# A new table for the order of work in a clustered-attention and feed-forward kernel on one core

## The chip, the cores and the metric

One Trainium2 chip (trn2), one core. The metric is the device time of one execution in microseconds (us). The inputs have fixed shapes and the program runs one launch.

## What is computed

The reference, cut to what matters:

```python
q_n, k_n, c_n = q/|q|, k/|k|, centroids/|centroids|            # q, k, v: [4, 8, 768, 64]
q_assign = argmax(q_n @ c_n.T); k_assign = argmax(k_n @ c_n.T)  # 16 clusters per head
scores = where(q_assign == k_assign, q @ k.T / 8, -1e9)
x = softmax(scores) @ v                                         # tokens x (heads * 64) = 3072 x 512
h = x @ w_in                                                    # 3072 x 2048
g = (a0 + a1*h + a2*h*h + a3*h*h*h) / (1 + |b0|*|h| + |b1|*h*h + 1e-6)
out = g @ w_out                                                 # 3072 x 512
```

## The kernel before

Work is tiled by batch b (0 to 3), head pair (0 to 3, two heads of 64 fill 128 partitions) and token block tb (0 to 2, 256 tokens each). Values that must keep more than 16 bits are split into a high and a low fp16 part, and TensorE (PE) adds the cross products.

- `load` steps: the weights come once, in 32 loads `rwi`, `rwo` through a ring of two buffers, and VectorE (DVE), ScalarE (ACT) and GpSimd (POOL) turn them into the resident fp16 pairs `win` and `wout`. This lies beside the attention of batch 0.
- `v_scale` loads the values of a batch once more (`rvm`, through the same two buffers) and squares them on ACT for a scale that only the batch's own feed-forward needs.
- `prep` loads a head pair's queries and keys (`rq`, `rk`), splits them (`tq`, `tk`), turns them by DMA into `sq` and `sk` (L1018), multiplies with the centroids into `ptl` (L1050), and builds the cluster marks on DVE: `mx`, `df`, `mxi`, `oh` (L1064 to L1074).
- `attend`, once per 128 tokens and head: scores `s` on PE (L1154), their scaling and row maximum on DVE (L1183), the exponential on ACT, the reciprocal of the sum on DVE (L1202), the split into `ah` on ACT (high) and DVE (low, L1214), the turn by DMA (L1221), and the product with the values, `px` (L1234), from which `x` comes. Batch 0 has a variant of its own, `attend_keys` (scores L1278 and L1322, product L1341).
- `moe`, once per batch and token block: for four chunks ci and two halves h, PE forms `ph` (two steps of 12 matmuls, L1441) in one of two PSUM buffers, ACT writes `u` = |h| scaled and `t`, DVE makes the polynomial in `t` (L1458, L1459) and so frees `ph`; POOL squares (`s`, L1505 and L1506), ACT takes Ln and Exp of it (L390, the helper of all its activations), the quotient is put together (L1517 or L1528, L1541, L1546), ACT casts the high part (L1550), the low part follows (L1554), and PE adds `po` (L1565). After four chunks ACT scales `po` into `ob`, and a DMA stores it. In batch 3 the low part and one more product run on DVE (`ed.3`, `gld.3` in the table K), and the second half's `u`, `t`, `s` tiles lie in space that attention lent: they are called `sq1`, `sk1`, `sq2` there and print as `sq`, `sk`, `sq`.

Every step is recorded with `plan.op` (L43); its engine name, its nanoseconds and its due time are dropped, and only the function that issues its instructions is kept. `emit` then runs the 4,184 functions in the order of the table `ORDER` (L61 to L244):

```python
    def emit(self):
        assert sorted(ORDER) == list(range(len(self.ops)))
        for i in ORDER:
            self.ops[i]()
```

Each engine, and SyncE (SP), which issues all loads, stores and turns, works off its own instructions in the order in which they were issued. So the table sets five queues at once, and with them the order in which the buffers of each ring change hands. A step at the head of a queue that must wait holds up all behind it on that engine.

Of the kernel before, what the change touches and what calls it, by code (L numbers as in the profile page):

```python
# [246 lines left out]
def clustered_attention_moe_kernel(  # L247
# [97 lines left out]

    def ring(dt, name):
        return buf([P, FW], dt, "ring", name, NR)

# [1306 lines left out]
```

## Time and profile before

| What | Value |
|---|---|
| median of 3 runs | 938.6 us (938.35 to 940.33) |
| the profiled execution | 938.91 us |
| its span, first to last instruction | 937.1 us |
| mean granted TensorE clock | 0.988 of full |
| busy: PE, DVE, ACT, POOL | 865.3, 840.7, 813.4, 729.5 us |
| DMA queue with the kernel's own transfers | 72.3% of 16 engines' span, 136.39 MB |

The profiled execution lies 0.31 us above the median, and 1.81 us of it lie outside the span. A page gives the busy time of each engine; matmuls overlap, so busy time of PE is a union of overlapping spans. The views used below are: stretches of time with the busy time of each engine in each, the instructions of one engine in order of time with the idle time before each in brackets and what ended it, the chain of work that ended last, and the waits by who waited for whom. "L390" is the line of the helper that issues every activation.

### The profile page before, as it was taken

The numbers are of one execution on the slowest core, as the hardware profiler recorded it, in microseconds if no ns is written. First come the engines' busy times: TensorE is split into PE (matmuls) and PEld (weight loads), VectorE is DVE, ScalarE is ACT, GpSimd is POOL, SyncE is SP. The second block draws the span as 40 slices with busy tenths as digits, with TensorE's granted clock in tenths as the row PEclk, the third lists the DMA queues.
The fourth block names the chain that finished last, engine by engine and source line by source line (L and its number), as shares of the span: only waits on it lengthen the run. The fifth ranks groups of instructions, "written<-read, shape, count | busy, mean of one in ns | idle before, by whom it ended". The sixth has DMA issues, their size and how long they took to land.

```text
span 937.1 us, 20745 instructions
## 1 busy us (share of the span) xinstructions
PE 865.3 (92%) x7705; PEld 583.9 (62%) x7705; DVE 840.7 (90%) x1503; ACT 813.4 (87%) x1558; POOL 729.5 (78%) x771
## 2 busy tenths in 40 slices
PE   2679998888999998999999999999999999998997
PEld 1357665665666666666666666666576765776663
DVE  6888989758989899999999999999999998998886
ACT  5577786999999999999999999999899998985764
POOL 3556788988999999989989898988878985454431
PEclk9989999999999999999999999999999999999999
DMA  7997755799867799988889888899787585610000
GB/s 224 240 205 149 213 138 162 190 206 205 163 121 153 151 155 199 189 145 165 156 153 175 155 158 168 158 176 192 141 154 145 103 154 113 106 29 12 12 24 22
DMA packets 360852, 137.70 MB, mean 147 GB/s; under 512 B 335664, under 2 KB 352048, under 8 KB 360752
## 3 DMA queue, kind: packets, MB, share of 16 engines
q1 hardware_dynamic: 360752, 136.39, 72.3%
q8 instruction: 60, 0.98, 0.4%
q14 instruction: 40, 0.33, 0.1%
HBM read 41.98 MB, written 6.29 MB: 52 GB/s over the span
## 4 chain that ended last, share of the span: by engine, by line
PE 51%; DVE 20%; ACT 11%; DMA 8%; issue 5%; POOL 4%; SPq 1%; ACTq 0%; DVEq 0%; POOLq 0%
PE ph L1441 17%; PE po L1565 16%; PE s L1154 6%; PE px L1234 6%; DVE ah L1214 3%; DVE s L1183 3%; DMA rwi<-in_moe_w_in_dram 2%; DVE t L1546 2%; ACT s L390 2%; DVE t L1458 2%; ACT u L390 1%; DVE t L1459 1%; DMA rvm<-in_v_dram 1%; DVE top L1287 1%; ACT ah L390 1%
## 5 line engine op out<-in xcount | busy, mean ns | idle before, releaser
L1441 PE MATMUL ph<-x,win 128*128 128x256 f16 x2304 | 274.0, 274 | 7.7 <-DVE t L1459 5.8
L1441 PEld LDWEIGHTS <-win 128*128 128x128 f16 x2304 | 225.2, 98 | 56.7 <-DVE t L1459 7.5
L1565 PE MATMUL po<-wout,s 128*128 128x512 f16 x1008 | 240.2, 380 | 0.1
L1565 PEld LDWEIGHTS <-s 128*128 128x128 f16 x1008 | 96.9, 98 | 102.4 <-issue 4.5
L1183 DVE TENSOR_SCALAR_CACHE_REDUCE s<-s,cc 128x768 f32<-128x768 f32 x144 | 146.3, 1019 | 15.9 <-PE s L1154 14.7
L1214 DVE SCALAR_TENSOR_TENSOR ah<-s,su,ah 128x768 f16<-128x768 f32 x144 | 144.4, 1010 | 2.8 <-ACT ah L390 2.3
L390 ACT ACTIVATE ah<-s,su 128x768 f16<-128x768 f32 x144 | 128.6, 901 | 8.9 <-DVE su L1202 8.3
L390 ACT ACTIVATE s<-s,nm 128x768 f32<-128x768 f32 x144 | 126.1, 876 | 8.1 <-DVE s L1183 6.2
L1154 PE MATMUL s<-sk,sq 128*128 128x384 f16 x576 | 117.4, 328 | 9.8 <-DVE ah L1214 8.1
L1506 POOL TENSOR_TENSOR s<-s,u 128x512 f32<-128x512 f32 x84 | 113.4, 1350 | 7.0
L1505 POOL TENSOR_SCALAR s<-u,g 128x512 f32<-128x512 f32 x84 | 71.9, 856 | 47.0 <-ACT u L390 32.8
L1528 POOL TENSOR_TENSOR s<-s,u 128x512 f32<-128x512 f32 x72 | 96.7, 1344 | 7.5 <-ACT u L390 7.1
L1554 POOL TENSOR_TENSOR s<-t,s 128x512 f16<-128x512 f32 x72 | 88.2, 1227 | 10.8 <-ACT s L1550 10.7
L1546 DVE SCALAR_TENSOR_TENSOR t<-s,t 128x512 f32<-128x512 f32 x84 | 85.1, 1014 | 0.5 <-POOL s L1528 0.4
L1154 PEld LDWEIGHTS <-sq 128*128 128x128 f16 x576 | 51.9, 98 | 54.0 <-DVE ah L1214 18.4
L1234 PE MATMUL px<-at,vhi 128*64 128x256 f16 x864 | 75.0, 275 | 1.5 <-DVE t L1459 1.0
L1459 DVE SCALAR_TENSOR_TENSOR t<-t,gk,ph 128x512 f32<-128x512 f32 x84 | 62.8, 748 | 3.0
L390 ACT ACTIVATE t<-ph,gk 128x512 f32<-128x512 f32 x84 | 65.4, 780 | 0.0
L390 ACT ACTIVATE u<-ph,gk 128x512 f32<-128x512 f32 x84 | 57.6, 686 | 7.1 <-PE ph L1441 6.5
L1458 DVE SCALAR_TENSOR_TENSOR t<-ph,gk,t 128x512 f32<-128x512 f32 x84 | 62.2, 741 | 1.0 <-ACT t L390 0.7
L1234 PE MATMUL px<-at,vlo 128*64 128x256 f16 x432 | 60.0, 273 | 0.0
L1535 POOL TENSOR_TENSOR t<-t,u 128x512 f32<-128x512 f32 x43 | 56.8, 1321 | 4.0 <-ACT u L390 0.6
(232 smaller groups left out, 1754.4 us busy)
## 6 DMA issues: line engine op xcount, KB each, us to landing
rwi<-in_moe_w_in_dram SPq DMA_DIRECT2D x16, 512.0 KB, 3.8
rwo<-in_moe_w_out_dram SPq DMA_DIRECT2D x16, 512.0 KB, 4.3
rk<-in_k_dram SPq DMA_DIRECT2D x32, 192.0 KB, 3.2
rq<-in_q_dram SPq DMA_DIRECT2D x32, 192.0 KB, 3.7
rvm<-in_v_dram SPq DMA_DIRECT2D x16, 384.0 KB, 4.1
rv<-in_v_dram SPq DMA_DIRECT2D x16, 384.0 KB, 4.3
...
```

The costliest lines, as they stand in the source:

```text
L390: lambda: nc.scalar.activation(out=out(), in_=in_(), func=func, **{a: (x() if callable(x) else x) for a, x in kw.items()}),
L1154: nc.tensor.matmul(sc.ap[:, i, :SH], lhsT=st["q" + x].ap[:, j, t, :], rhs=st["k" + x].ap[:, j, ks, :].rearrange("p t c -> p (t c)"), start ...
L1183: lambda nm=nm, view=view: ts(out=view(), in0=view(), scalar1=cc.ap[:, 0:1], scalar2=None, op0=ALU.mult, op1=ALU.min, accum_out=nm.ap),
L1214: lambda part=part, view=view, su=su: stt(out=part(1), in0=view(), scalar=su.ap, in1=part(0), op0=ALU.mult, op1=ALU.subtract),
L1234: nc.tensor.matmul(px.ap[j * D : (j + 1) * D, :], lhsT=vv.ap[:, j, kt, :], rhs=at[j].ap[:, p_, kt].rearrange("p t c -> p (t c)"), start=(i ...
L1441: nc.tensor.matmul(ph.ap[:, fi * TW : (fi + 1) * TW], lhsT=win[:, wpart, c, f * P : (f + 1) * P], rhs=xs[c].ap[:, xpart], start=(i == 0), ...
L1458: stt(out=t[h].ap, in0=ph.ap, scalar=col("rho")(), in1=t[h].ap, op0=ALU.mult, op1=ALU.mult)
L1506: nc.gpsimd.tensor_tensor(out=sv(), in0=sv(), in1=uv(), op=ALU.mult)
L1528: lambda uv=uv, sv=sv: nc.gpsimd.tensor_tensor(out=sv(), in0=sv(), in1=uv(), op=ALU.mult),
L1546: lambda tv=tv, sv=sv: stt(out=tv(), in0=sv(), scalar=2.0, in1=tv(), op0=ALU.subtract, op1=ALU.mult),
L1554: lambda tv=tv, g16=g16, e=(nc.vector if kshare("gld", b, i_) else nc.gpsimd): e.tensor_tensor(out=g16(1), in0=tv(), in1=g16(0), op=ALU.su ...
L1565: nc.tensor.matmul(po[ti].ap, lhsT=g16(gg)[:, c0 : c0 + P], rhs=wout[:, wpart, f, :], start=(i == 0 and f == 0), stop=(i == 2 and f == NF ...
```

## The change

The table `ORDER` is replaced by another permutation of the same 4,184 steps. Its first line, old and new:

```diff
-3 377 376 28 375 4 5 374 6 7 40 8 9 1 379 381 382 29 383 32 30 10 388 31 391 380 34 33 392 41 384 44 42 489
...
+3 376 377 28 375 374 4 5 6 40 7 8 0 9 379 381 382 10 29 383 32 30 388 31 391 380 33 34 392 44 384 41 490 42
```

Besides, the nanoseconds that each step is recorded with are others (a weight load 2000 in place of 1460, a load of values 1500 for 1100, of queries or keys 800 for 1100, and some compute steps by a few per cent). `Plan.op` drops them, so the program does not hold them. Code behind four new switches (`mw`, `swing`, `atc`, `fine`) is added; none of them is in the table K, whose line is unchanged, so it takes the path of before:

```diff
-    def dma(ns, out, in_, r, w, vt, chain=None):
-        op("SP", ns, lambda: nc.sync.dma_start(out=out(), in_=in_()), r, w, vt, co=w, chain=chain)
+    def dma(ns, out, in_, r, w, vt, chain=None, claim=()):
+        op("SP", ns, lambda: nc.sync.dma_start(out=out(), in_=in_()), r, w, vt, claim=claim, co=w, chain=chain)
...
-            raw = buf([P, 2 * FW], I32, "wraw", "r" + n, 2)
-            dma(1460, lambda raw=raw: raw.ap, lambda src=src: src.bitcast(I32), [], [raw], vt - kn("wd", 3))
+            raw = load([P, 2 * FW], I32, "r" + n)
+            dma(2000, lambda raw=raw: raw.ap, lambda src=src: src.bitcast(I32), [], [raw], vt - kn("wd", 3))
...
-                        (750, 1280)[k] if last else (900, 1600)[k],
+                        (750, 1280)[k] if last else (930, 1780)[k],
```

Each engine has the same compute and DMA instructions in both programs; the waits between engines follow from the order. 227 of the 4,184 steps keep their place in the table; a step is moved by 12 places on average. Lines below L345 of the changed file stand 5 to 11 further down than before.

Three places, as the queues stand before and now. The first is SP, from the second value load of batch 1's scale to the loads of its third head pair: `sk11_1` and `sq11_1` are the turned keys and queries of head pair 1 of batch 1, `rvm2_0` and `rvm2_1` values of batch 2 for its scale, `rk1_2` keys of the next pair. Before:

```order
L404 DMA rvm2_0_2645<-in_v_dram 128x2x384
L1026 DMA sk21_0_2537<-sk11_0_2181 64x1536
L404 DMA rv1_0_2657<-in_v_dram 128x2x384
L1018 DMA_TRANSPOSE sk11_1_2692<-tk11_1_2300 128x12x128
L404 DMA rvm2_1_2702<-in_v_dram 128x2x384
L1018 DMA_TRANSPOSE sq11_1_2709<-tq11_1_2454 128x12x128
```

Now:

```order
L409 DMA rk1_2_2679<-in_k_dram 128x384
L409 DMA rvm2_0_2690<-in_v_dram 128x2x384
L1026 DMA_TRANSPOSE sq11_1_2696<-tq11_1_2466 128x12x128
L1026 DMA_TRANSPOSE sk11_1_2703<-tk11_1_2324 128x12x128
L409 DMA rvm2_1_2709<-in_v_dram 128x2x384
```

The two turns now follow each other, and the value load that stood between them stands behind both.

The second is DVE where the first feed-forward steps begin: `t0_0_0_0` and `t0_0_0_1` are the polynomials of the first two `ph`, `mxi1_1` and `oh1_1` the cluster marks of head pair 1 of batch 1, `ah` and `s` its attention. Before:

```order
L1073 TENSOR_REDUCE mxi1_1_2956<-df1_1_2890 128x24
L1183 TENSOR_SCALAR s1_0_1_1_2940,nm1_0_1_1_2976<-s1_0_1_1_2940,cc1_0_1787 128x2x384
L1202 RECIPROCAL su1_0_1_0_2915<-su1_0_1_0_2915 128x1
L1074 TENSOR_TENSOR oh1_1_2988<-df1_1_2890,mxi1_1_2956 128x384
L1458 SCALAR_TENSOR_TENSOR t0_0_0_0_2985<-ph0_0_0_0_2896,gk0_2308,t0_0_0_0_2985 128x512
L1459 SCALAR_TENSOR_TENSOR t0_0_0_0_2985<-t0_0_0_0_2985,gk0_2308,ph0_0_0_0_2896 128x512
L1002 SCALAR_TENSOR_TENSOR tk11_2_2883<-rk1_2_2728,ksc1_2_2948,tk11_2_2883 128x12x64
L1202 RECIPROCAL su1_0_1_1_3002<-su1_0_1_1_3002 128x1
L1214 SCALAR_TENSOR_TENSOR ah1_0_1_0_3041<-s1_0_1_0_2872,su1_0_1_0_2915,ah1_0_1_0_3041 128x768
L1214 SCALAR_TENSOR_TENSOR ah1_0_1_1_3047<-s1_0_1_1_2940,su1_0_1_1_3002,ah1_0_1_1_3047 128x768
L953 TENSOR_SCALAR qsc1_2_3067<-sumq1_2_2974 128x1
L1183 TENSOR_SCALAR s1_0_2_1_3057,nm1_0_2_1_3069<-s1_0_2_1_3057,cc1_0_1787 128x2x384
```

Now:

```order
L1191 TENSOR_SCALAR s1_0_1_1_2947,nm1_0_1_1_2962<-s1_0_1_1_2947,cc1_0_1777 128x2x384
L1222 SCALAR_TENSOR_TENSOR ah1_0_1_0_2958<-s1_0_1_0_2877,su1_0_1_0_2917,ah1_0_1_0_2958 128x768
L961 TENSOR_SCALAR qsc1_2_2997<-sumq1_2_2937 128x1
L1467 SCALAR_TENSOR_TENSOR t0_0_0_0_2980<-ph0_0_0_0_2897,gk0_2307,t0_0_0_0_2980 128x512
L1468 SCALAR_TENSOR_TENSOR t0_0_0_0_2980<-t0_0_0_0_2980,gk0_2307,ph0_0_0_0_2897 128x512
L1010 SCALAR_TENSOR_TENSOR tk11_2_2912<-rk1_2_2679,ksc1_2_2953,tk11_2_2912 128x12x64
L1210 RECIPROCAL su1_0_1_1_2983<-su1_0_1_1_2983 128x1
L1191 TENSOR_SCALAR s1_0_2_0_3003,nm1_0_2_0_3035<-s1_0_2_0_3003,cc1_0_1777 128x2x384
L1467 SCALAR_TENSOR_TENSOR t0_0_0_1_3029<-ph0_0_0_1_2964,gk0_2307,t0_0_0_1_3029 128x512
L1468 SCALAR_TENSOR_TENSOR t0_0_0_1_3029<-t0_0_0_1_3029,gk0_2307,ph0_0_0_1_2964 128x512
L1222 SCALAR_TENSOR_TENSOR ah1_0_1_1_3051<-s1_0_1_1_2947,su1_0_1_1_2983,ah1_0_1_1_3051 128x768
```

The marks (`mxi1_1`, `oh1_1`) have left this place; they stand 14 and 15 steps further down. Between the two polynomials stood two `ah` and one `s` step of the attention; now one `ah` stands ahead of the first polynomial, the other behind the second, and one `s` step, of another row of tokens, is left between them. On PE the score step of `s1_0_2_0` has come ahead of the third `ph` (`ph0_0_1_0`), that of `s1_0_2_1` has gone behind the first half of the fourth (`ph0_0_1_1`), and the first product `px1_0_0` stands 6 steps further down. On ACT the squares of two `rvm` loads of batch 2 (steps 2217 and 2219 of the table) stand 27 and 30 steps further down.

The third is ACT in batch 3, where the last chunk of token block 0 ends: `sq13_0_3`, `sk13_0_3`, `sq23_0_3` are its `u`, `t`, `s`, and the cast into `sq23_0_3` is what the last `po` of the block waits for; `sq23_1_0` belongs to the next block. Before:

```order
L390 ACTIVATE sq13_1_0_12350<-ph3_1_0_1_12296,gk3_8970 128x512
L390 ACTIVATE sk13_1_0_12353<-ph3_1_0_1_12296,gk3_8970 128x512
L390 ACTIVATE sq23_1_0_12355<-sq23_1_0_12355,cq_76 128x512
L390 ACTIVATE u3_2_0_0_12393<-ph3_2_0_0_12336,gk3_8970 128x512
L390 ACTIVATE t3_2_0_0_12399<-ph3_2_0_0_12336,gk3_8970 128x512
L1550 CAST sq23_0_3_12260<-sk13_0_3_12263 128x512
```

Now:

```order
L395 ACTIVATE sq13_1_0_12296<-ph3_1_0_1_12236,gk3_9080 128x512
L395 ACTIVATE u3_1_0_0_12249<-s3_1_0_0_12251,cq_76 128x512
L1560 CAST sq23_0_3_12207<-sk13_0_3_12194 128x512
L395 ACTIVATE u3_1_3_0_12332<-ph3_1_3_0_12281,gk3_9080 128x512
L395 ACTIVATE t3_1_3_0_12336<-ph3_1_3_0_12281,gk3_9080 128x512
L395 ACTIVATE u3_1_0_0_12249<-u3_1_0_0_12249 128x512
L395 ACTIVATE sq23_1_0_12321<-sq23_1_0_12321,cq_76 128x512
```

The cast stood behind the step that reads POOL's square of the next block, `sq23_1_0`; it now stands ahead of it.

## Rows read from the trace of the kernel before

**Rows 1.** The page: busy time, share of the span and instructions of each engine.

```profile
PE 865.3 (92%) x7705; PEld 583.9 (62%) x7705; DVE 840.7 (90%) x1503; ACT 813.4 (87%) x1558; POOL 729.5 (78%) x771
```

**Rows 2.** Four stretches: length, busy time by engine (instructions), clock, DMA share, GB/s.

```profile
0.00:200.00 200.00, 156.83 (x1817) 110.64 (x1817) 163.39 (x340) 147.61 (x272) 141.74 (x181) 0.97 0.78 192
200.00:235.00 35.00, 28.97 (x267) 20.91 (x264) 29.02 (x55) 32.90 (x71) 30.40 (x33) 0.95 0.88 199
235.00:843.00 608.00, 592.92 (x5071) 398.52 (x5070) 575.27 (x1012) 576.04 (x1125) 522.80 (x531) 1.00 0.81 149
843.00:937.00 94.00, 86.57 (x558) 53.87 (x556) 73.03 (x99) 56.87 (x94) 34.55 (x28) 0.98 0.05 18
```

**Rows 3.** Waits from 0 to 200 us: who for whom, total us, times, longest.

```profile
ACT mwi L390 <- DMA rwi<-in_moe_w_in_dram: 10.9, 9, 2.3
...
ACT mwo L390 <- DMA rwo<-in_moe_w_out_dram: 7.3, 3, 2.9
```

**Rows 4.** PE in order of time, 199 to 229 us: start, us, instruction, [idle before].

```profile
201.71 0.76 PE L1050 MATMUL ptl<-cen,sq 128*128 128x16 f16 x24 [1.68 <-DMA sq<-tq]
...
212.07 2.79 PE L1441 MATMUL ph<-x,win 128*128 128x256 f16 x24 [1.16 <-DVE t L1459]
214.91 1.75 PE L1154 MATMUL s<-sk,sq 128*128 128x384 f16 x8
218.55 7.08 PE L1441 MATMUL ph<-x,win 128*128 128x256 f16 x48 [1.89 <-DVE t L1459]
226.64 0.41 PE L1234 MATMUL px<-at,vhi 128*64 128x256 f16 x4 [1.01 <-DVE t L1459]
```

**Rows 5.** SP in order of time, 186 to 196 us.

```profile
193.74 0.91 SPq L404 DMA_DIRECT2D rvm<-in_v_dram  x1
```

**Rows 6.** The chain that ended last, 120 to 205 us: start, us, what.

```profile
194.71 6.96 DMA sq<-tq
```

**Rows 7.** DVE in order of time, 203 to 221 us.

```profile
208.03 0.53 DVE L1073 TENSOR_REDUCE mxi<-df 128x24 bf16<-128x384 bf16 x1
...
209.49 1.08 DVE L1074 TENSOR_TENSOR oh<-df,mxi 128x384 f16<-128x384 bf16 x1
...
213.84 1.94 DVE L1214 SCALAR_TENSOR_TENSOR ah<-s,su,ah 128x768 f16<-128x768 f32 x2 [0.73 <-ACT ah L390]
...
215.75 1.02 DVE L1183 TENSOR_SCALAR_CACHE_REDUCE s<-s,cc 128x768 f32<-128x768 f32 x1
```

**Rows 8.** Three-microsecond stretches at the clock's lower level; columns as in rows 2.

```profile
219.00:222.40 3.40, 3.40 (x19) 2.42 (x17) 3.18 (x7) 3.01 (x8) 2.54 (x3) 0.51 1.15 219
860.80:864.10 3.30, 3.30 (x16) 2.01 (x14) 3.23 (x5) 2.40 (x5) 1.96 (x2) 0.50 0.22 82
```

**Rows 9.** ACT in order of time, 204 to 221 us.

```profile
206.18 0.83 ACT L390 ACTIVATE rvm<-rvm 128x768 f32<-128x768 f32 x1
...
216.82 0.84 ACT L390 ACTIVATE rvm<-rvm 128x768 f32<-128x768 f32 x1
```

**Rows 10.** PE in order of time, 850 to 870 us.

```profile
858.72 0.61 PE L1565 MATMUL po<-wout,sq 128*128 128x512 f16 x2 [1.57 <-ACT sq L1550]
860.24 1.41 PE L1565 MATMUL po<-wout,sq 128*128 128x512 f16 x4 [0.91 <-DVE sq L1554]
```

**Rows 11.** ACT in order of time, 845 to 866 us.

```profile
856.20 0.72 ACT L390 ACTIVATE sq<-sq,cq 128x512 f32<-128x512 f32 x1 [5.48 <-POOL sq L1506]
...
858.06 0.61 ACT L1550 CAST sq<-sk 128x512 f16<-128x512 f32 x1
```

**Rows 12.** All engines in order of time, 848 to 858 us.

```profile
849.29 0.69 DVE L1517 SCALAR_TENSOR_TENSOR s<-s,u 128x512 f32<-128x512 f32 x1
...
850.14 4.67 POOL L1505 TENSOR_SCALAR sq<-sq,g 128x512 f32<-128x512 f32 x1 [5.62 <-ACT sq L390]
...
853.57 0.69 DVE L1546 SCALAR_TENSOR_TENSOR t<-s,t 128x512 f32<-128x512 f32 x1
```

**Rows 13.** Line L1505 in batch 3's second halves: count, min/median/max ns, first and last start.

```profile
L1505 POOL TENSOR_SCALAR sq<-sq,g x12: 692/744/4669, 805.0 to 921.7; 128x512 f32<-128x512 f32 x12
```

More of the change, by code (lines that the diff above doesn't have):

```diff
@@ L347, in ring, with load @@
         return buf([P, FW], dt, "ring", name, NR)
+    MERGE = bool(kn("mw"))
+    def load(shape, dt, name):
+        return buf(shape, dt, "ring", name, NR) if MERGE else buf(shape, dt, "wraw", name, 2)
     def wide(name):
@@ L647, in weights_wide @@
                     src = moe_w_out[(4 * i + c) * P : (4 * i + c + 1) * P, :]
-                raw = buf([P, 2 * FW], I32, "wraw", "r" + n, 2)
+                raw = load([P, 2 * FW], I32, "r" + n)
                 raws.append(raw)
-                dma(1460, lambda raw=raw: raw.ap, lambda src=src: src.bitcast(I32), [], [raw], vt - kn("wd", 3))
+                dma(2000, lambda raw=raw: raw.ap, lambda src=src: src.bitcast(I32), [], [raw], vt - kn("wd", 3))
                 def high(raw=raw):
@@ L684, in weights_wide @@
             op(
-                "POOL", 2300,
+                "POOL", 2430,
                 lambda w=w, mag=mag: nc.gpsimd.tensor_tensor(
@@ L745, in weights_wide @@
             op(
-                "POOL", 2100,
+                "POOL", 2180,
                 lambda part=part, wf=wf: nc.gpsimd.tensor_tensor(out=part(1), in0=wf(), in1=part(0), op=ALU.subtract),
@@ L754, in load_v @@
     def load_v(b, hp, why, vt):
-        t = buf([P, 2, NT * D], F32, *(("rv", f"rv{b}_{hp}", kn("rvn", 1)) if why == "u" else ("wraw", f"rvm{b}_{hp}", 2)))
+        if why == "u":
+            t = buf([P, 2, NT * D], F32, "rv", f"rv{b}_{hp}", kn("rvn", 1))
+        else:
+            t = load([P, 2, NT * D], F32, f"rvm{b}_{hp}")
         dma(
-            1100, lambda: t.ap,
+            1500, lambda: t.ap,
             lambda: v[b, 2 * hp : 2 * hp + 2].rearrange("h (p t) d -> p h (t d)", t=NT), [], [t], vt, "v" + why,
@@ L883, in prep @@
                 dma(
-                    1100,
+                    800,
                     lambda t=raw[nm], j=j: t.ap[:, j],
@@ L1000, in prep @@
                 dve(
-                    1471,
+                    1580 if GW == 2 else 1471,
                     lambda nm=nm, sc=sc, hi=hi, lo=lo: stt(
@@ L1037, in fixed_rows @@
                 nc.gpsimd.memset(rows("q2"), 0.0)
-            op("POOL", 579, fixed_rows, [], [tm["k2"], tm["q2"]], vt + kb("p2", b, 2))
+            op("POOL", 1100, fixed_rows, [], [tm["k2"], tm["q2"]], vt + kb("p2", b, 2))
         for x in ("k1", "q1"):
@@ L1073, in prep @@
         dve(541, lambda: nc.vector.tensor_reduce(out=mx2.ap, in_=df.ap, axis=AX.X, op=ALU.max), [df], [mx2], u)
-        dve(622, lambda: tt(out=oh.ap, in0=df.ap, in1=spread(mx2), op=ALU.is_equal), [df, mx2], [oh], u)
+        dve(900 if GW == 2 else 640, lambda: tt(out=oh.ap, in0=df.ap, in1=spread(mx2), op=ALU.is_equal), [df, mx2], [oh], u)
         if "q2" not in tm:
@@ L1083, in mark @@
                 )
-            op("POOL", 1100, lambda: (mark(0, -MASK), mark(1, 0.0)), [oh], [marks[0]], u)
+            op("POOL", 830, lambda: (mark(0, -MASK), mark(1, 0.0)), [oh], [marks[0]], u)
         else:
@@ L1403, in moe @@
         xs = [xt[b, tb, c] for c in range(NCC)]
-        po2 = bank([P, TB, DM], F32, "o", f"po{b}_{tb}", 1)
+        swing = b == B - 1 and tb % 2 and kn("swing")
+        po2 = bank([P, TB, DM], F32, "s" if swing else "o", f"po{b}_{tb}", 2 if swing else 1)
         po = [half(po2, ti) for ti in range(TB)]
@@ L1422, in moe @@
                 if h % GW == 0:
-                    if last and GW == 2 and ci % 2:
+                    if last and GW == 2 and ci in kn("atc", (1, 3)):
                         tiles = [buf([P, GW, FW], F32, "at", f"{m}{n}", kn("at", 3)) for m in "uts"]
@@ L1461, in moe, with view @@
                 dve(1523, poly, [ph, gk], [t[h]], u_ + h + kb("phr", b), [t_t], n=2)
-                if (h + 1) % GW:
+                gw = 1 if last and ci >= NWC - 1 and tb >= NB - kn("fine", 0) else GW
+                if (h + 1) % gw:
                     continue
-                seg = list(u)
-                k = GW - 1
+                seg = list(u) if gw == GW else [h]
+                k = gw - 1
                 i_ = ((b * NB + tb) * NWC + ci) * 2 // GW + h // GW
                 us, tss, ss = ([w_[h] for h in seg] for w_ in (u, t, s))
-                def view(w_):
-                    return w_.ap.rearrange("p h c -> p (h c)")
+                def view(w_, gw=gw, h=h):
+                    return w_.ap.rearrange("p h c -> p (h c)") if gw == GW else w_.ap[:, h]
                 def uv(view=view, u_t=u_t):
@@ L1506, in square @@
                         nc.gpsimd.tensor_tensor(out=sv(), in0=sv(), in1=uv(), op=ALU.mult)
-                    op("POOL", (2375, 3600)[k], square, [*us, g1], ss, uu + kb("sq", b), [s_t, u_t])
+                    op("POOL", (2330, 3930)[k], square, [*us, g1], ss, uu + kb("sq", b), [s_t, u_t])
                 acq = kshare("acq", b, i_)
@@ L1515, in moe @@
                     dve(
-                        (840, 1300)[k] if last else (1000, 1800)[k],
+                        (840, 1300)[k] if last else (1000, 1850)[k],
                         lambda uv=uv, sv=sv, acq=acq: stt(out=sv(), in0=sv(), scalar=0.0 if acq else 1.0 + 1e-6, in1=uv(), op0=ALU.add, op1=ALU.mult),
@@ L1521, in moe @@
                     if not acq: op(
-                        "POOL", (820, 1250)[k],
+                        "POOL", (790, 1340)[k],
                         lambda sv=sv: nc.gpsimd.tensor_scalar(out=sv(), in0=sv(), scalar1=cq, scalar2=1.0, op0=ALU.add, op1=ALU.mult),
@@ L1526, in moe @@
                     op(
-                        "POOL", (1400, 2250)[k],
+                        "POOL", (1360, 2440)[k],
                         lambda uv=uv, sv=sv: nc.gpsimd.tensor_tensor(out=sv(), in0=sv(), in1=uv(), op=ALU.mult),
@@ L1535, in times @@
                         nc.gpsimd.tensor_tensor(out=tv(), in0=tv(), in1=uv(), op=ALU.mult)
-                    op("POOL", (2183, 3350)[k], times, [*us, gk], tss, uu + kb("mul", b), [t_t, u_t])
+                    op("POOL", (2183, 3840)[k], times, [*us, gk], tss, uu + kb("mul", b), [t_t, u_t])
                 else:
                     dve(
-                        (919, 1380)[k] if last else (1146, 2000)[k],
+                        (919, 1600)[k] if last else (1110, 2100)[k],
                         lambda tv=tv, uv=uv, col=col: stt(out=tv(), in0=tv(), scalar=col("a0")(), in1=uv(), op0=ALU.add, op1=ALU.mult),
@@ L1544, in moe @@
                 dve(
-                    (840, 1220)[k] if last else (1100, 1700)[k],
+                    (800, 1290)[k] if last else (1080, 1930)[k],
                     lambda tv=tv, sv=sv: stt(out=tv(), in0=sv(), scalar=2.0, in1=tv(), op0=ALU.subtract, op1=ALU.mult),
@@ L1552, in moe @@
                 op(
-                    *(("DVE", (780, 1350)[k]) if kshare("gld", b, i_) else ("POOL", (1231, 2080)[k])),
+                    *(("DVE", (780, 1400)[k]) if kshare("gld", b, i_) else ("POOL", (1231, 2230)[k])),
                     lambda tv=tv, g16=g16, e=(nc.vector if kshare("gld", b, i_) else nc.gpsimd): e.tensor_tensor(
@@ L1573, in moe @@
                            u_ + h + kb("po", b, 4.0), [po2, s_t])
+        whole = load([P, TB, DM], F32, f"ob{b}_{tb}") if MERGE else None
         for ti in range(TB):
-            ob = buf([P, DM], F32, "wraw", f"ob{b}_{tb}_{ti}", 2)
+            ob = half(whole, ti) if MERGE else load([P, DM], F32, f"ob{b}_{tb}_{ti}")
             act(693, lambda ob=ob: ob.ap, lambda ti=ti: po[ti].ap, AF.Identity, [po[ti], g1], [ob],
-                vt + NG - 1 + kb("ob", b, 1.0), [po2], scale=lambda: g1.ap[:, OI : OI + 1])
+                vt + NG - 1 + kb("ob", b, 1.0), [po2, *([whole] if MERGE else [])], scale=lambda: g1.ap[:, OI : OI + 1])
             dma(
-                750,
+                1100,
                 lambda ti=ti: out[b * S : (b + 1) * S].rearrange("(p t) d -> p t d", t=NT)[:, tb * TB + ti, :],
-                lambda ob=ob: ob.ap, [ob], [], vt + NG,
+                lambda ob=ob: ob.ap, [ob], [], vt + NG, claim=[whole] if MERGE else (),
             )
```

8 lines of the change are left out of this document (4 added, 4 removed), and 360 rows, old and new, of the table ORDER.

## The prediction

> **What bounds the kernel now.** I read the busy times first, then the same by stretch, then the idle gaps of the engine that ends last, and followed each gap to what ended it.
>
> The page gives no single bound: PE is busy 92%, DVE 90%, ACT 87% [rows 1]. By stretch it is clearer [rows 2]. From 235 to 843 us, 608 us long, PE is idle for 608.0 - 592.9 = 15.1 us, DVE for 32.7 and ACT for 32.0: three engines keep one pace, and a better order can take at most the 15.1 us there. In the last 94 us POOL and ACT have run out of work, and PE alone (86.6 us busy) sets the end. In the first 200 us, batch 0's attention and the weights, PE is idle for 43 us, but nothing can fill that: no feed-forward step can start before batch 0's first `x`, and ACT waits there for weight loads, 10.9 + 7.3 us [rows 3]. Two places remain in which PE waits for an order that could be another: the handover from attention to feed-forward (200 to 235 us) and the end of token block 0 in batch 3 (857 to 861 us).
>
> **The change, part by part.** The instructions are the same, so the work costs what it cost; what can change is who waits. The recorded nanoseconds reach no instruction. The sum is made against the profiled 938.9 us; the median, 938.6, lies 0.3 below.
>
> *Head, to 200 us: 0.* The first weight loads keep their slots on SP or move by one, and the first `ph` is the 171st step of PE in both tables. What hides any shuffle there is the chain of loads; if it went, the 18.2 us of ACT's waits [rows 3] would be at stake. I take 0, ends -3 and +3, a sixth of these waits either way.
>
> *The two turns on SP.* PE waits 1.68 us for the turned queries [rows 4], issued at 194.71 and landed 6.96 us later [rows 6]. Ahead of them SP issued a value load for 0.91 us [rows 5], which now stands behind both turns. PE needs both, so the later one comes 0.9 earlier: -0.9, ends 0 and -1.7 (the whole wait).
>
> *The polynomials on DVE.* A third `ph` needs the PSUM buffer that the first polynomial frees. PE waits 1.16 us for it, then 1.89 for the second, then 1.01 for a later one [rows 4]. Ahead of the first polynomial the marks go (0.53 + 1.08 us) and one `ah` comes (half of 1.94, 0.97) with a small scale step that I leave out [rows 7]: some 0.5 earlier. PE also does one score step, half of 1.75 = 0.9 us [rows 4], before it asks. 0.5 + 0.9 covers 1.16: gone. Between the polynomials both `ah` (1.94) have gone, so the second comes 0.5 + 1.9 = 2.4 earlier; PE asks 0.9 sooner, for a score step went behind. 1.5 of 1.89 is covered: -1.5. The third wait stood before `px`, now six steps further down: -1.0. Together -3.7; ends 0 (each wait replaced by another) and -4.1 (all three gone).
>
> *The clock there.* The granted clock falls to 0.51, its lower level of 1.2 GHz, for 3.4 us right behind the second wait [rows 8]; work at half speed costs half of it, 1.7 us. If the wait goes I take the drop as gone: -1.7, ends 0 and -1.7.
>
> *What the handover gives back.* These three make -6.3. But ACT is busy for 32.9 of the 35 us there [rows 2], so the stretch can shrink only by what ACT is spared: 2.1 us of idle time and the two squares of `rvm`, 0.83 + 0.84 [rows 9], pushed 27 and 30 steps down. That is 3.8 at most, and the squares must then be done in the next stretch, beside its 32 us of ACT idle time. I keep half of 6.3: **-3.2**. What is late next is ACT.
>
> *The cast in batch 3.* PE waits 1.57 us for a cast on ACT and 0.91 for the DVE step behind it [rows 10]. The cast was not late itself: ACT stood 5.48 us before a step that reads POOL's square of the next block, and the cast was issued behind it at 858.06 [rows 11]. It now stands ahead of that step. Its input came from DVE steps of 0.69 us that ended by 854.3 [rows 12]. So both waits go, 2.5 us, and with them the drop of the clock behind them, half of 3.3 [rows 8], 1.6. PE ends the kernel, so nothing takes this back: **-4.1**, ends 0 and -4.1.
>
> *The middle, 235 to 843 us: 0.* Most steps have moved there, by a dozen places, without a trend that I could read: of PE's gaps about as many consumers came nearer to their producer as went away. Ends: -5 (a third of the 15.1 us of idle time) and +5 (as much again).
>
> Sum: -3.2 - 4.1 = -7.3, so 938.9 - 7.3 = 931.6, I say **931.5 us**.
>
> **A row and a rule.** POOL's square of the next block took 4.67 us; its like take 0.744 at the median [rows 13]. Beside it DVE ran products and sums of two operands without a gap from 849.29 to 854.26 [rows 12], and POOL's step ended 0.6 us later: it stood still while DVE ran. So 3.9 us of the wait in the last place were lost on POOL, not queued on ACT. The Trainium skill, page "SBUF — State Buffer", section "Who interferes with whom", states that a DVE instruction with two SBUF inputs contends with a GpSimd instruction that reads SBUF. The trace agrees, with that 4.67 us. By the row the sum stays 931.5, since the cast no longer waits behind the square. By the rule every closed run of such DVE steps in batch 3 can stop POOL, and a table made with fixed durations would pack DVE tighter: the time would be that of the second rival.
>
> **The rivals.** *More arrives.* The middle gives a third of its idle time (-5) and the handover keeps all it could (-3.1 more): 931.5 - 8 = 923.5. For it: the 15.1 us are there to be had. Against: DVE and ACT are 95% busy beside them [rows 2]. Chance 0.20.
>
> *Slower: POOL stopped in batch 3.* Place: the squares (L1505) of batch 3's three blocks, each at the head of a chain to `po`. Price of one: 4.67 - 0.74 = 3.9 us, and 1.7 for the clock behind PE's wait, 5.6 in all. One eats most of the gain (937.1); it decides from the second on: 931.5 + 11.2 = 942.7, slower than before. For it: DVE makes the quotient there alone, in steps of 0.69 us that stand closely together. Against: of 12 such squares the median is 0.744, so one in 12 was stopped for long [rows 13]. Chance 0.24.
>
> *No change.* The table may do nothing that counts: the pace of ACT and DVE in the middle swallows the handover, and in batch 3 another step is the late one. Then 938.9 less at most half of the second place's 4.1: 937 to 939, say 938. Against: the cast's wait is undone by one move in one queue. Chance 0.13.
>
> **How the numbers follow.** Forecast 0.43, more 0.20, no change 0.13, slower 0.24. A measurement of this kernel tells about 0.2% (1.9 us) from no change. The forecast and "more" lie below that line: faster 0.63, same 0.13, slower 0.24. The range: low end 938.9 - 6.3 (all of the handover) - 4.1 - 5 (middle) - 3 (head) = 920.5, say 920; high end the second rival, 942.7, say 943. The forecast's own range, with the handover at 0 or at 6.3 and half of the ends of middle and head, is 924.5 to 939.
>
> **What would show it.** Right: PE's waits for `t` between 205 and 230 us are below 1 us in sum, the clock stays up there, and the cast of block 0 in batch 3 comes ahead of the wait for POOL with no gap of PE at the block's end. The handover is half kept if the first `po` of batch 0 comes 2 to 4 us sooner. Wrong: new gaps of PE between 235 and 843 us, above 20 us in sum, or squares of POOL above 2 us in batch 3 with PE idle behind them, or a first `ph` later than 204 us, by which the head was not neutral.

## The result and the profile after

| | before | after | ratio, 95% interval |
|---|---|---|---|
| first comparison | 939.47 us (938.35 to 942.9, 4 runs) | 928.66 us (927.74 to 932.17, 4 runs) | 0.9895, 0.9872 to 0.9917 |
| again, beside the last experiments | 939.05 us (11 runs) | 928.68 us (927.95 to 930.56, 5 runs) | 0.9885, 0.9864 to 0.9906 |

The changed kernel is 1.1% faster, some 10.4 us. One run of the kernel before, 1,271.5 us at a granted clock of 0.66, is left out of every comparison. The forecast was 931.5 us, 2.8 us too slow, and inside its range. The profiled execution of the changed kernel took 932.17 us (span 930.4), the slowest of its four, so the times of its profile lie about 3.5 us above the median. The page's busy line, and the four stretches with the columns of [rows 2]:

```profile
PE 863.5 (93%) x7705; PEld 581.1 (62%) x7705; DVE 835.6 (90%) x1503; ACT 811.2 (87%) x1558; POOL 729.3 (78%) x771
```

```profile
0.00:200.00 200.00, 156.05 (x1757) 108.69 (x1759) 163.79 (x336) 146.24 (x270) 138.82 (x176) 0.97 0.77 193
200.00:235.00 35.00, 31.30 (x333) 23.07 (x329) 29.38 (x58) 33.37 (x69) 29.09 (x36) 0.98 0.71 166
235.00:843.00 608.00, 593.87 (x5070) 397.88 (x5071) 568.31 (x1014) 576.13 (x1130) 529.61 (x534) 1.00 0.80 150
843.00:930.40 87.40, 82.25 (x549) 51.47 (x547) 74.09 (x98) 55.49 (x91) 31.77 (x26) 0.99 0.08 23
```

Against [rows 1, 2] PE is busy for 1.8 us less and its span is 6.7 us shorter; DVE is busy for 5.1 us less with the same instructions. The two tables finish the same work at other times, so stretches that are fixed in us do not compare like with like. I therefore count in PE's own steps: PE does 801 steps of the table in both programs, step 170 is the first `ph`, and in before step 199 lies at 242 us, step 240 at 287, step 680 at 777, step 720 at 822. At each of these both programs have done the same steps of PE. At step 200 they have not: the changed kernel has done one `po` step (six matmuls, 1.3 us) more. What each part took, in us, in the profile of before, in the profiled execution of after, and in the second profile of the changed kernel (the run "again"):

| Part | before | after | again |
|---|---|---|---|
| start to step 170 | 204.3 | 206.3 | 200.8 |
| 170 to 199, the handover | 37.8 | 36.5 | 36.5 |
| 199 to 240 | 45.1 | 45.9 | 45.9 |
| 240 to 680, the middle | 489.6 | 485.3 | 486.5 (a drop of the clock at 470 in it) |
| 680 to 720 | 45.1 | 45.6 | 45.6 |
| 720 to the last step, 800 | 109.3 | 105.0 | 105.0 |

Steps 170 to 240, then 240 to 680, in before, after and "again", and last steps 170 to 240 in "lock", a run below that has before's order there and no drop of the clock; columns as in [rows 2]:

```profile
204.32:287.24 82.92, 77.57 (x647) 53.11 (x648) 75.58 (x136) 80.22 (x161) 76.53 (x77) 0.98 0.77 155
206.26:288.69 82.43, 76.01 (x647) 51.95 (x647) 74.59 (x137) 80.17 (x163) 76.96 (x80) 1.00 0.75 150
200.83:283.25 82.42, 76.01 (x647) 51.93 (x648) 74.57 (x137) 80.16 (x163) 76.96 (x80) 1.00 0.81 159
...
287.24:776.88 489.64, 475.69 (x4096) 317.93 (x4094) 465.29 (x833) 468.92 (x922) 440.11 (x455) 1.00 0.87 161
288.69:774.00 485.31, 474.41 (x4095) 316.83 (x4093) 458.81 (x833) 467.20 (x923) 441.96 (x454) 1.00 0.87 161
283.25:769.76 486.51, 475.73 (x4095) 317.59 (x4093) 459.90 (x833) 467.50 (x923) 441.95 (x454) 1.00 0.87 161
...
206.50:289.00 82.50, 76.26 (x648) 52.17 (x648) 76.24 (x136) 80.41 (x162) 77.32 (x77) 1.00 0.79 157
```

So the time came from the middle and from the end, in "again" also from the head, but not from the handover: 1.3 us were gained there by step 199, and 0.5 of them were left at step 240, less than the 1.7 us of the clock's drop that of these three only before's profile has there. PE's idle time from step 170 to 240 went up, from 82.92 - 77.57 = 5.4 to 82.43 - 76.01 = 6.4 us. PE's waits in the handover of the changed kernel, in order of time (start, us, instruction, idle time before it in brackets), which answer to [rows 4]:

```profile
214.19 2.79 PE L1450 MATMUL ph<-x,win 128*128 128x256 f16 x24 [0.35 <-DVE t L1468]
217.75 1.48 PE L1450 MATMUL ph<-x,win 128*128 128x256 f16 x12 [0.77 <-DVE t L1468]
222.46 2.79 PE L1450 MATMUL ph<-x,win 128*128 128x256 f16 x24 [1.26 <-DVE t L1468]
227.08 2.33 PE L1575 MATMUL po<-wout,s 128*128 128x512 f16 x10 [0.75 <-POOL s L1564]
...
235.41 0.82 PE L1162 MATMUL s<-sk,sq 128*128 128x384 f16 x4 [0.43 <-DVE ah L1222]
...
240.15 2.78 PE L1450 MATMUL ph<-x,win 128*128 128x256 f16 x24 [0.67 <-DVE vm L779]
```

Three waits for `t`, 1.16 + 1.89 + 1.01 = 4.06 us, have become three of 0.35 + 0.77 + 1.26 = 2.38 us, one for POOL of 0.75, and two for other DVE steps of 0.43 + 0.67. That is 4.23 us, so the waits have moved and not gone. In the end PE waits for next to nothing: it is busy for 74.74 of the 75 us from 843 to 918 us. POOL's square of the next block (L1505 before, L1515 now), which answers to [rows 12], and the line's durations, which answer to [rows 13]:

```profile
846.07 1.64 POOL L1515 TENSOR_SCALAR sq<-sq,g 128x512 f32<-128x512 f32 x1 [3.50 <-ACT sq L1560]
```

```profile
L1515 POOL TENSOR_SCALAR sq<-sq,g x12: 691/863/1642, 804.9 to 914.9; 128x512 f32<-128x512 f32 x12
```

ACT in order of time there, which answers to [rows 11]:

```profile
845.39 0.61 ACT L1560 CAST sq<-sk 128x512 f16<-128x512 f32 x1
...
849.10 0.72 ACT L395 ACTIVATE sq<-sq,cq 128x512 f32<-128x512 f32 x1
```

The cast comes ahead of the step that reads POOL's square, as the table says, and that step waits for nothing: POOL's square took 1.64 us where it had taken 4.67. The clock in the profiled execution fell to its lower level for 6.8 us behind a wait at 193.9 us; columns as in [rows 8]:

```profile
194.24:201.07 6.83, 6.48 (x28) 3.42 (x29) 4.39 (x11) 5.74 (x14) 6.32 (x10) 0.50 1.03 255
```

Half of 6.8 us, 3.4, is about what this execution lies above the median. Behind the handover the clock no longer falls before the last 2.3 us.

### The profile page after: what moved, and what is told of

The parts are those of the page before. It is cut to its first block, busy times and chain, and to the rows that moved or that the text cites. A ratio compares the mean times of both kernels' runs of the same rounds, so it can differ in the third digit from the quotient of the medians.

```text
span 930.4 us, 20764 instructions
## 1 busy us (share of the span) xinstructions
PE 863.5 (93%) x7705; PEld 581.1 (62%) x7705; DVE 835.6 (90%) x1503; ACT 811.2 (87%) x1558; POOL 729.3 (78%) x771
## 4 chain that ended last, share of the span: by engine, by line
PE 54%; DVE 19%; ACT 9%; POOL 6%; issue 6%; DMA 5%; SPq 1%; ACTq 0%; DVEq 0%; POOLq 0%
PE ph L1450 18%; PE po L1575 18%; PE s L1162 7%; PE px L1242 5%; DVE ah L1222 3%; DVE s L1191 3%; DMA rvm<-in_v_dram 2%; PE s L1286 2%; DVE t L1467 1%; DVE t L1556 1%; ACT s L395 1%; PE px L1349 1%; DVE t L1468 1%; DVE top L1295 1%; PE z L1330 1%
## 5 line engine op out<-in xcount | busy, mean ns | idle before, releaser
L1516 POOL TENSOR_TENSOR s<-s,u 128x512 f32<-128x512 f32 x84 | 114.4, 1362 | 7.0
L1538 POOL TENSOR_TENSOR s<-s,u 128x512 f32<-128x512 f32 x72 | 99.1, 1378 | 7.0 <-ACT u L395 6.7
L1515 POOL TENSOR_SCALAR s<-u,g 128x512 f32<-128x512 f32 x84 | 69.6, 829 | 36.4 <-ACT u L395 33.6
L1556 DVE SCALAR_TENSOR_TENSOR t<-s,t 128x512 f32<-128x512 f32 x84 | 81.8, 973 | 0.8 <-POOL s L1538 0.5
```

The costliest lines, as they stand in the source:

```text
L1516: nc.gpsimd.tensor_tensor(out=sv(), in0=sv(), in1=uv(), op=ALU.mult)
L1538: lambda uv=uv, sv=sv: nc.gpsimd.tensor_tensor(out=sv(), in0=sv(), in1=uv(), op=ALU.mult),
L1556: lambda tv=tv, sv=sv: stt(out=tv(), in0=sv(), scalar=2.0, in1=tv(), op0=ALU.subtract, op1=ALU.mult),
```

## The experiments

In all of them only the table differs; in "again" nothing does. Step numbers in the diffs are those of the table. Each was timed in five rounds beside the kernel before.

| Run | median, us (runs) | ratio to before, 95% interval | mean granted clock |
|---|---|---|---|
| tail | 937.98 (12) | 0.9989, 0.9969 to 1.0009 | 0.9889 |
| handover | 939.62 (12) | 1.0003, 0.9985 to 1.0022 | 0.9892 |
| middle | 939.65 (12) | 1.0008, 0.9992 to 1.0023 | 0.9872 |
| head | 937.85 (12) | 0.9993, 0.9975 to 1.0011 | 0.9913 |
| midtail | 932.60 (7) | 0.9942, 0.9919 to 0.9964 | 0.9884 |
| headhand | 935.50 (12) | 0.9969, 0.9952 to 0.9985 | 0.9916 |
| cast | 936.22 (12) | 0.9984, 0.9968 to 1.0001 | 0.9893 |
| lock | 936.83 (12) | 0.9981, 0.9967 to 0.9995 | 0.9892 |
| again | 928.68 (5) | 0.9885, 0.9864 to 0.9906 | 0.9928 |
| early | 929.45 (6) | 0.9900, 0.9877 to 0.9923 | 0.9923 |
| squares | 932.33 (6) | 0.9921, 0.9901 to 0.9942 | 0.9917 |
| both | 930.56 (6) | 0.9911, 0.9887 to 0.9936 | 0.9923 |

The kernel before has 75 runs beside these: 935.18 to 944.79 us, median 938.7, mean clock 0.9892. Its runs differ by 9.6 us, and the slower ones tend to have the lower clock: a straight line through the 75 gives 0.65 us less for each 0.001 more of the mean clock (correlation -0.76, so it accounts for somewhat over half of the variance).

### Four parts alone: tail, handover, middle, head

Each has the new order in one part of the table and before's order elsewhere. The first changed line of each:

```diff
 tail (from step 3800)
-3828 3757 3782 3775 3816 3857 3829 3776 3807 3777
+3828 3757 3782 3200 3773 3857 3775 3807 3776 3777
...
 handover (steps 870 to 1050)
-802 1231 1408 361 803 1290 2214 814 362 1232 1409 804 1291 790 816 373
+802 1231 1408 361 803 1290 2214 814 362 1232 1409 804 373 1535 1534 790
...
 middle (steps 1050 to 3800)
-1676 1316 880 1317 867 906 1336 1549 1345 881
+1676 1316 880 906 907 1345 1336 867 1346 868
...
 head (the first 870 steps)
-3 377 376 28 375 4 5 374 6 7 40 8 9 1 379 381
+3 376 377 28 375 374 4 5 6 40 7 8 0 9 379 381
```

> The table of before up to its step 3800 (about 808 us), the new order from there to the end. Theory (the prediction's term for the cast in batch 3, stretched to the whole tail): 4.1 us faster than before, about 934.5, because the cast of block 0 stands ahead of the wait for POOL: PE has no gap of over 0.5 us between 850 and 865 us, and the clock does not fall there. Rival (the gain lies in the middle alone, the tail only ends what was sooner begun): within 1 us of before, 938 to 940.

> The new order only for the steps 870 to 1050 of the table of before (about 194 to 233 us), before's order on both sides. Theory (the prediction's handover): PE's waits for the polynomials and the drop of the clock at 219 us go, half of the 6.3 us is kept: 3.2 us faster, about 935.5. Rival (what the profile of the changed kernel suggests: its lead of 2.3 us at PE's step 183 was gone at step 200): the gain is given back to ACT and DVE within 20 us, within 1 us of before, 938 to 940.

> The new order only for the steps 1050 to 3800 of the table of before (about 233 to 808 us), before's head, handover and end. Theory (the prediction): the moves there cancel, within 1 us of before. Rival (from the trace of the changed kernel, where PE gained 4.8 us between its steps 200 and 680): 3 to 6 us faster, 933 to 936, with PE's gaps behind its step 600 gone and no drop of the clock at 670 us.

> The new order only for the first 870 steps of the table of before (to about 194 us). Theory (the prediction): the chain of weight loads hides every shuffle, within 1 us of before, 938 to 940, and the first feed-forward step of PE starts at 204 us as before. Rival (from the trace of the changed kernel, in which that step came 2.0 us later behind a wait of 1.48 us and a half clock of 6.8 us at 194 us): 2 to 3 us slower, 941 to 942.

None of the four is told from before by its time; the four medians add up to -1.3 us, and the whole change has -10.4. The profiles say why. In "middle" PE's steps 240 to 680 took 486.7 us against 489.6: 2.9 us quicker, nearly as in "again". Then steps 680 to 720 took 48.1 us against 45.1, which took it all back: at the seam where before's order begins again stood this wait (PE in order of time):

```profile
807.88 0.82 PE L1154 MATMUL s<-sk,sq 128*128 128x384 f16 x4 [2.37 <-DVE sk L1459]
```

In "tail" the steps from 720 on took 105.9 us, 3.4 less than before, with a wait of 0.8 us behind the seam among them. That is near to its theory, but 1.7 of it is a drop of the clock that before's profile has there; the time over 12 runs shows 1.1 us. A part that is cut out of a table was laid out for what stood around it.

In "handover" steps 170 to 200 (the same steps as in before) took 37.5 us, against 37.9, though the drop of the clock is missing: PE's idle time there grew from 4.2 to 5.4 us. Its rival was right in the outcome; it compared before and after at step 200, where the changed kernel has done a `po` step more. In "head" the first `ph` came at 204.8 us, neither earlier nor later.

### Two halves: midtail and headhand

```diff
 midtail (from step 1050)
-1676 1316 880 1317 867 906 1336 1549 1345 881
+1676 1316 880 906 907 1345 1336 867 1346 868
...
 headhand (the first 1050 steps)
-3 377 376 28 375 4 5 374 6 7 40 8 9 1 379 381
+3 376 377 28 375 374 4 5 6 40 7 8 0 9 379 381
```

> The table of before up to its step 1050 (about 233 us), the new order from there to the end, so that middle and tail have no seam between them. Theory (the seam at 808 us took back what the middle had won: in the run 'middle' PE was 4.0 us ahead at its step 680 against its step 200, and a wait of 2.5 us stood behind the seam): 4 + 4 = 8 us faster than before, about 931. Rival (the parts add: the middle alone and the tail alone measured +0.6 and -1.1): within 1 us of before, 938 to 940.

> The new order for the first 1050 steps of the table of before (to about 233 us), before's order from there. Theory (ACT is the bound of the handover: busy 36.4 to 36.8 us of the 37.5 to 37.9 us between PE's steps 170 and 200 in three traces): within 1.5 us of before, 937.5 to 940.5; PE's steps 170 to 200 take 37.5 to 38.5 us. Rival (the handover's gain needs the new head in front of it): 3 us faster, about 936.

With one seam each, the halves measure -5.4 us (0.9942 of 938.6) and -2.9 us (0.9969), together -8.3, which lies within the interval of the whole, -12.0 to -7.8. So middle and end carry about two thirds of these 8.3 us, the head with the handover behind it the rest. "midtail" lies between its theory (8 us) and its rival (within 1 us); its steps 240 to 680 took 486.5 us and those from 720 on 105.0, as in "again". "headhand" was faster than its theory allowed and as fast as its rival said, but not by the handover: its steps 170 to 200 took 37.7 us. Its first `ph` came at 201.7 us.

### The cast alone, and the run of DVE that kept POOL out: cast and lock

```diff
 cast
-3966 3913 3945 3903 4056 3934 4059 4057 3915 4019 3997 3916 3935
+3966 3913 3903 3934 3915 3916 3945 4056 4059 4057 4019 3997 3935
...
 lock
-3966 3913 3945 3903 4056 3934 4059 4057 3915 4019 3997 3916 3935 3902 3917 3946 3936 3998 3919 4020 3943 3947
+3943 3966 3913 3945 3903 4056 3934 4059 4057 3915 4019 3997 3916 3935 3902 3917 3946 3936 3998 3919 4020 3947
```

> The table of before with one change: the cast of block 0 in batch 3 (step 3916) and the DVE step before it stand ahead of the ACT step that waits for POOL's square (step 3945) and of the two ACT steps behind that one. Theory (the prediction's term): PE's waits of 1.57 and 0.91 us at the end of block 0 go: 2.5 us faster, 4.1 where the clock fell behind them, so 935 to 936.6. Rival (another step is late there at once): a new wait of PE of over 1 us between 850 and 870 us, within 1 us of before.

> The table of before with one DVE step moved: the polynomial of the next block (step 3943, 1.52 us, one of its inputs in PSUM) goes into the middle of the closed run of eight DVE steps with two SBUF operands, beside which POOL's square took 4.67, 4.68, 4.45 and 4.67 us in the four traces that have this run. The cast stays behind the ACT step that waits for POOL. Theory (DVE's run keeps POOL out, and POOL gets in at the first other step): the square takes 2.5 us or less, ACT's wait of 5.48 us falls below 3.5, the cast comes about 2.5 us sooner and PE's two waits shrink to below 0.5: 2 to 4 us faster. Rival (the square is slow for another reason, its own operands or the DMA): it takes over 4 us again, and PE's waits stay.

In "cast" the cast came at 853.47 us, and PE's two waits for it were gone. One of nearly the same size took their place. PE, then ACT, then POOL, each in order of time:

```profile
856.77 1.46 PE L1565 MATMUL po<-wout,sq 128*128 128x512 f16 x6
858.06 1.47 PE L1441 MATMUL ph<-x,win 128*128 128x256 f16 x12
861.54 1.46 PE L1565 MATMUL po<-wout,sq 128*128 128x512 f16 x6 [2.01 <-ACT ob L390]
```

```profile
853.47 0.62 ACT L1550 CAST sq<-sk 128x512 f16<-128x512 f32 x1 [2.98 <-DVE sk L1546]
856.30 0.72 ACT L390 ACTIVATE sq<-sq,cq 128x512 f32<-128x512 f32 x1 [2.21 <-POOL sq L1506]
...
860.81 0.68 ACT L390 ACTIVATE ob<-po,g 128x512 f32<-128x512 f32 x1
```

```profile
849.92 4.67 POOL L1505 TENSOR_SCALAR sq<-sq,g 128x512 f32<-128x512 f32 x1 [5.61 <-ACT sq L390]
```

POOL's square took 4.67 us as before, ACT still waited for it until 856.3, and now `ob`, which PE's next `po` waits for, was among the steps behind. PE's waits at the place fell from 1.57 + 0.91 = 2.48 to 2.01 us: the cast's place in ACT's queue was worth 0.5 us of PE's waiting, not 2.5.

"lock" leaves the cast behind that wait and breaks the closed run of DVE steps. POOL, then DVE, then PE:

```profile
851.95 1.68 POOL L1505 TENSOR_SCALAR sq<-sq,g 128x512 f32<-128x512 f32 x1 [5.60 <-ACT sq L390]
```

```profile
852.38 0.69 DVE L1517 SCALAR_TENSOR_TENSOR s<-s,u 128x512 f32<-128x512 f32 x1
852.98 0.74 DVE L1458 SCALAR_TENSOR_TENSOR sk<-ph,gk,sk 128x512 f32<-128x512 f32 x1
853.76 0.75 DVE L1459 SCALAR_TENSOR_TENSOR sk<-sk,gk,ph 128x512 f32<-128x512 f32 x1
854.43 1.11 DVE L1546 SCALAR_TENSOR_TENSOR t<-s,t 128x512 f32<-128x512 f32 x1
```

```profile
858.80 0.59 PE L1565 MATMUL po<-wout,sq 128*128 128x512 f16 x2
860.10 1.04 PE L1565 MATMUL po<-wout,sq 128*128 128x512 f16 x4 [0.71 <-DVE sq L1554]
```

The square ended at 853.63 us, 0.65 after the first DVE step with an input in PSUM began. In before it ended at 854.81, 0.55 after the last step of the run; in "cast" at 854.59, 0.55 after; in the changed kernel at 847.71, 0.55 after the run gave way to a polynomial at 847.16. Each time that is a square's own 0.69 us, or a little less, counted from the end of the run. PE's waits fell from 2.48 to 0.71 us, and its last 80 steps took 105.7 us against 107.1 in "cast" and 107.7 in "handover", which has before's end and no drop of the clock in it. The time, 0.9981, is below 1 with its whole interval, some 1.8 us, a little less than the 2 to 4 expected. By time "cast" (0.9984) and "lock" are not told apart; what each move is worth is read from PE's waits in one profile each. That DVE's run holds POOL's square is shown and its rival falls: across the profiles the longest square of batch 3's second halves is 4.45 to 4.69 us in the six that have the closed run (before, handover, middle, head, headhand, cast) and 1.64 to 1.84 us in the other eight. The Trainium skill's page "SBUF — State Buffer", section "Who interferes with whom", says that a DVE step with two inputs in SBUF contends with a GpSimd step that reads SBUF, and that one with at most one such input does not, outside DVE's two-port modes: the trace agrees with both halves, with the 4.67 and the 1.68 us.

### The changed kernel once more, and three variants: again, early, squares, both

```diff
 early
-1971 2541 2423 2235 1958 2424 2418 1943 1957 2425 2542 2426 2419 1972 2427 1946
+1971 2541 2423 2235 2424 2418 1943 2425 2542 2419 2426 2427 1958 1957 1972 1946
...
 squares
-846 3202 835 1312 874 848 2216 836
+846 835 1312 874 848 836
...
-1414 1329 2217 1545 1342 1415 839 1330 877 1343 2218 1331
+1414 1329 1545 1342 1415 839 1330 877 1343 1331
```

In "squares" the removed steps, with the load 3207, the square 3204 with its load 3205, and the steps 2219 to 2222 that follow, stand 12 to 105 places further down; "both" has the two edits together.

> The changed kernel once more, as it is, so that the three variants of it beside this run have their base on the same chip. If its first four runs (927.74 to 932.17 us) stand for it, the median is 927 to 930 and the mean granted clock 0.993 to 0.995. The wait of 2.14 us of PE at 475 us, which stood in the same place in three profiles with this middle, is there again; the half clock of 6.8 us at 194 us need not be.

> The changed kernel with one move on DVE at 472 us: the product into t of block 1 of batch 1 (step 1958, 1.64 us) goes behind the two low parts of head pair 1 of batch 2 (steps 2419 and 2427), and the reciprocal and the maximum (2425, 2542) come ahead of it. PE's score step waits for the first of these low parts. Theory (PE's wait is a matter of order): the wait of 2.14 us falls below 0.8, the drop of the clock behind it goes where there was one: 1.5 to 3 us faster than the run 'again'. Rival (DVE has no idle time there, so it sets the pace and PE waits a few steps later): the wait goes, but new ones of 1 us or more stand between 480 and 550 us, and the time is within 1 us of 'again'.

> The changed kernel with three of ACT's squares of the values for the scales (steps 3202, 2217, 2219, 0.84 us each) and the loads between them moved from 217, 225 and 237 us to about 238, 245 and 253 us, so that ACT is spared 1.7 us, and with its own idle time of 1.2 us 2.5 us, between PE's steps 170 and 200. Theory (ACT is the bound of the handover): these 30 steps of PE take 35.3 to 36.5 us, against 37.8 in the changed kernel's profile. Rival (ACT only keeps step with DVE and PE there): they take 37.3 to 38.3 us. The time moves by less than 1.5 us in either case, for the squares are done in the next stretch.

> The moves of 'early' and 'squares' together in the changed kernel. If both theories hold, 2 to 4 us faster than 'again', about 925; if the pace of the three engines takes both back, within 1 us of 'again'.

"again" repeats the first result. In "early" the wait at 470 us fell from 2.15 to 0.70 us, and a new one stood 8 us further on. PE in "again", then in "early":

```profile
470.23 2.58 PE L1162 MATMUL s<-sk,sq 128*128 128x384 f16 x8 [2.15 <-DVE ah L1222]
```

```profile
469.97 1.75 PE L1162 MATMUL s<-sk,sq 128*128 128x384 f16 x8 [0.70 <-DVE ah L1222]
478.00 0.82 PE L1162 MATMUL s<-sk,sq 128*128 128x384 f16 x4 [1.39 <-DVE ah L1222]
```

0.70 + 1.39 is 2.09: the rival was right, the wait only moved, and the time is that of "again" within its interval.

"squares" shows that ACT's load does not bound the handover. The stretch from PE's step 170 to 200 (the same steps in these two), in "again", then in "squares", columns as in [rows 2]:

```profile
200.80:238.60 37.80, 33.36 (x265) 23.72 (x266) 33.96 (x62) 36.58 (x76) 34.89 (x38) 1.00 0.82 172
```

```profile
205.70:243.50 37.80, 33.36 (x265) 23.70 (x266) 33.96 (x61) 35.19 (x73) 34.89 (x38) 1.00 0.66 131
```

ACT is spared 1.4 us and the stretch is as long as it was, with PE's waits the same to 0.02 us. PE in "squares", then DVE, then ACT:

```profile
217.18 1.49 PE L1450 MATMUL ph<-x,win 128*128 128x256 f16 x12 [0.76 <-DVE t L1468]
218.50 0.81 PE L1162 MATMUL s<-sk,sq 128*128 128x384 f16 x4
219.15 1.47 PE L1450 MATMUL ph<-x,win 128*128 128x256 f16 x12
221.88 2.36 PE L1450 MATMUL ph<-x,win 128*128 128x256 f16 x20 [1.25 <-DVE t L1468]
```

```profile
219.35 1.02 DVE L1191 TENSOR_SCALAR_CACHE_REDUCE s<-s,cc 128x768 f32<-128x768 f32 x1 [0.49 <-PE s L1162]
220.29 0.14 DVE L1191 DVE_READ_ACCUMULATOR s<-s,cc 128x1 f32 x1
220.29 0.74 DVE L1467 SCALAR_TENSOR_TENSOR t<-ph,gk,t 128x512 f32<-128x512 f32 x1
```

```profile
218.84 0.77 ACT L395 ACTIVATE t<-ph,gk 128x512 f32<-128x512 f32 x1
```

ACT had finished `t` at 219.61 us, but the polynomial that frees the buffer began at 220.29, behind a scale step of the attention that itself waited for a score of PE, and PE made that score behind a `ph` that had waited for the polynomial before. Read so, the stretch is a loop from PE through DVE back to PE, over two PSUM buffers; in this pass ACT's step in it was done 0.68 us before DVE turned to it. By the medians "squares" is 3.6 us slower than "again" all the same, where less than 1.5 was expected: PE got a new wait of 1.99 us at 245 us, with the clock at half for 3.4 us behind it, and in the profile another drop at 194. What would break the loop, the polynomial ahead of the scale step, was not tried, so the loop is an account of these rows and not shown by an experiment. "both" lies 1.9 us above "again", with the same wait of 1.98 us behind step 200. No variant beats the changed kernel.

## Why the prediction came out as it did

The time was right (931.5 against 928.7), the terms only in part; errors of opposite sign, 2.7 us too much in the handover and 5 to 6 too little in head and middle, cancelled in part. That the number came so near is luck in that measure.

**What bounds the kernel.** Three engines at one pace with 15.1 us of idle time of PE to be had [rows 2], and PE alone in the last stretch: this held. The changed kernel's PE idles for 608.0 - 593.9 = 14.1 us from 235 to 843 us.

**Head, 0 with ends of 3.** Within its ends, but probably not zero. The first `ph` came at 200.8 to 206.3 us in the seven profiles with the new head (mean 203.5) and at 204.3 to 207.8 in the seven with the old one (mean 205.5): 2.0 us, by order and clock together, and a difference that the scatter of 5.4 us within the new head makes uncertain. The mean clock of "head" and "headhand" is higher than before's, too (0.9913 and 0.9916 against 0.9892). What I named as the test, a first `ph` later than 204 us, did come true in the one profiled execution (206.3), and would have misled: it was the drop at 194 us of that execution.

**The two turns, the polynomials, the handover: -3.2.** Wrong: steps 170 to 240 take 82.9 us before and 82.4 after, a gain of 0.5 that is less than the missing drop of the clock, and 82.5 us in "lock", which has the old order and no drop of the clock in that place. To step 199 the new order is 0.8 us ahead of "lock" (36.5 against 37.3 us), and it loses that again. The step that failed is that each wait goes: I moved each consumer against its producer as if the others stood still. The waits of 1.16 and 1.89 us did shrink, and others came, 2.38 + 0.75 + 0.43 + 0.67 in place of 4.06 us. The second failed step is "What is late next is ACT": I read a bound off a busy share (32.9 of 35 us), and "squares" took 1.4 us from ACT without any effect. My test, waits for `t` below 1 us in sum, failed with 2.38. My other sign, the first `po` 2 to 4 us sooner, came true in excess (225.7 against 230.4 us) and meant nothing, for that `po` stands three PE steps earlier in the new order. Of the three terms the two turns alone held: the wait of 1.68 us is gone in every profile that has both the new head and the new handover. It lies ahead of the first `ph` and so counts in the head above.

**The clock.** Two terms, 1.7 and 1.6 us, took a drop seen once for a sure one. The same wait of 1.89 to 1.90 us in the handover is followed by half clock in before, tail, midtail and cast, and not in lock; the wait at the end of block 0, 1.36 us or more, in before, head and headhand, and not in handover and middle. So a drop came in four of five and in three of five executions, seven of ten together: such a term is a chance times a price. From step 170 to 200 none of the seven profiles with the new handover has a drop, against four of the seven with the old one.

**The cast in batch 3: -4.1.** Right in size: from step 720 to the end 109.3 us before and 105.0 after, 4.3 less, of which 1.7 are the clock and the rest the two waits. Against an end without the drop (107.7 us in "handover") it is 2.7. Wrong in cause: I wrote that the cast need only stand ahead of the step that waits for POOL. "cast" shows that alone to be worth 0.5 us, because `ob` and the other ACT steps stay behind that wait; "lock" shows the other move, POOL let in between DVE's steps, to be worth 1.8 us with the cast left where it was. The new table does both. The step that failed is "So both waits go", as far as the cast's own place was to do it.

**The middle, 0 with ends of 5.** Within its ends: 489.6 us before, 485.3 and 486.5 after. By the busy times of exactly that stretch PE idles for 489.64 - 475.69 = 13.95 us before, for 485.31 - 474.41 = 10.90 after and for 486.51 - 475.73 = 10.78 in "again". So 3.1 us are idle time of PE; the other 1.3 us, in the profiled execution alone, are busy time, near the 1.7 that the drop at 670 us costs before's profile; this one has no drop there, and "again" has one at 470. I had looked only for a trend in distances and found none; that was too little to say zero. Which of the moves there took the 3.1 us off was not separated and stays open.

**The rivals.** The result lies between the forecast and "more arrives" (923.5): of that rival's two parts the middle came in large part, 3.1 to 4.3 of 5 us, and the handover not at all. "Slower" did not come: with the new order the longest square of batch 3's second halves is 1.64 us; its mechanism, though, was the real one, working in before. "No change" fell.
